# Attention followed by a two-expert layer: four experts of half 0 first, gathered row tiles last, eight store tiles

## The chip, the cores and the metric

The kernel runs on one core of a Trainium2 chip. The metric is the device time of one execution in microseconds. Of the kernel before, four runs are known: 454.48, 451.84, 455.76 and 464.94 us, a median of 455.12 us. One execution was recorded by the hardware profiler; its time is 454.48 us, and the span from its first to its last profiled instruction is 452.6 us, so 1.9 us lie around the span. All times of day below ("at 208.8") are microseconds from the start of that span.

## The reference, cut to what matters

Causal attention in blocks of 64 over q, k, v of 8 batches x 8 heads x 576 positions x 64; its output, with the heads side by side, is x of 4608 tokens x 512. A noisy router picks two of eight experts per token. Each expert is two matrix products with a ReLU between.

```python
attn = softmax(mask(scale * q @ k.T)) @ v          # mask: block_i >= block_j, blocks of 64
x = attn.transpose(0, 2, 1, 3).reshape(B * S, H * D)
noisy = x @ w_gate + log1p(exp(x @ w_noise)) * noise
top2, top2_w = two largest of noisy per token, softmax over the two
for e in range(8):
    for k in range(2):
        mask = top2[:, k] == e
        h = np.maximum(x[mask] @ w1[e], 0.0)        # 512 -> 1024
        out[mask] += top2_w[mask, k, None] * (h @ w2[e])   # 1024 -> 512
```

## The kernel before, in words

**Attention and router.** The batches go in four groups g = 0 to 3 of two batches (1152 tokens, nine tiles of 128 rows). A counter of slots, 26 for a group (UG), paces everything: `at(slot, fn, ...)` files a call, `run(slot)` makes the calls of a slot. Groups 0 and 1 are half 0 of the tokens, groups 2 and 3 half 1. For each group the router gives every token two row numbers, one in each of its two experts' blocks, and `scatter` (L496, an indirect DMA issued by GpSimd, L499) writes a tile of token rows to such rows of a DRAM buffer, `xd[0]` or `xd[1]`: 18 scatters a group. A block has CAP = 640 rows, five row tiles of 128. Rows of tokens for which the expert is the higher-numbered of the two stand at the low end of the block, the others at its high end. `LT[e]` = 0, 1, 2, 3, 3, 4, 5, 5 is how many of expert e's five row tiles, from the low end, may hold rows of the first kind.

**Expert blocks.** Sixteen blocks b = 0 to 15 follow, one for each pair (half, expert), in the order of the list `SEQ` (L626): (0,0) (0,1) (0,2) (1,0) (1,1) (1,2), then (0,3) (1,3) (0,4) (1,4) and so on. "Layer1(b,f)" is `layer1` (L567): eight steps f = 0 to 7 a block, each 4 x 2 matmuls of 320 columns (L574) and one ReLU on ScalarE (L577). "Layer2(b,c)" is `layer2` (L581): five steps c = 0 to 4, one for each row tile, each eight matmuls of 512 columns (L586). The PSUM tile `yp` of such a step is one of two; it is read by ScalarE, which scales it by the router's weight into a tile `ysb` (L591, one of four) that a DMA stores to `yd[half]` (L593); expert 7 has no such store. For c < LT[e] VectorE also reads it: `yo` = yp x weight + `yg` (L596), and an indirect DMA of GpSimd scatters `yo` to the output (L598). `yg` holds the partner rows of the same tokens, fetched from `yd` of the same half by `gather` (L609, an indirect DMA of GpSimd, L614), so it can only be fetched when the stores of all lower experts of the half have landed. Ten `yg` tiles go round.

**Order of the work.** The whole program is in an order written by hand (`steps`, L823): layer1(b,1..7), layer1(b+1,0), layer2(b,0..4), and so on; after every step one more slot is run. What goes with a step:

- `load_x` (L515) reads the block's 640 rows of `xd`, transposed, into `xg` (three tiles) by a DMA on SP's queue (L519). It waits until every scatter of that half has landed. Blocks 0, 1 and 2 are loaded at slots 3*UG+18 to 3*UG+21, block 3 (the first of half 1) at layer1(2,1), block b+2 at layer1(b,1) from there on (`XL`, L833).
- `load_rec` and `read_rec` fetch and work out the row numbers and weights of a half; those of half 1 at layer1(2,1) and layer1(3,3).
- `load_w` (L220, issued at L232) loads one expert's w1 and w2 in four parts k = 0 to 3 of 512 KB, in bf16, by plain DMAs of GpSimd. Experts 0, 1, 2 come during attention and blocks 0 and 1 (pools `wE`, `wM`); expert 3 at blocks 3 and 4, expert 4 at 5 and 6, and so on (`WL`, L813).
- Gathers: block 1's at layer1(1,1); blocks 2 to 8 at steps 2, 3, 4, 6, 7 of the block's own layer 1 (`GJ`); from block 9 on in the block ahead (`GS`).
- The 18 scatters of group 3, the last of half 1, are filed for slots 118 to 135, one a slot, which are the steps of blocks 0 and 1. GpSimd issues scatters, gathers, output scatters and weight loads in one order; each of its DMAs also waits for its eighth predecessor's landing (one of eight semaphores).

Of the kernel before, what the change touches and what calls it, by code (L numbers as in the profile page):

```python
# [9 lines left out]
BF16 = mybir.dt.bfloat16  # L10
# [9 lines left out]
def kernel(  # L20
# [15 lines left out]
    N, Dm = out.shape  # L36
    E = moe_w_gate.shape[1]
    F = moe_w1.shape[2]
    assert Dm == H * D and N == B * S
    P = 128  # L40
# [5 lines left out]
    NH = 2  # L46
    TH = NT // NH
    CAP = 640
    CT = CAP // P
# [8 lines left out]
    LT = (0, 1, 2, 3, 3, 4, 5, 5)  # L58
# [5 lines left out]
    UG = 2 * UN  # L64
# [32 lines left out]
    wE = main.enter_context(tc.tile_pool(name="wE", bufs=2))  # L97
# [6 lines left out]
    top = main.enter_context(ExitStack())  # L104
# [115 lines left out]
    def load_w(pool, e, k=None):  # L220

        if k in (None, 0, "a"):
            wload[e] = (pool.tile([P, DB, F], BF16, tag="w1", name="w1sb"),
                        pool.tile([P, FB, Dm], BF16, tag="w2", name="w2sb"))
        for i, (t, src) in enumerate(zip(wload[e], (moe_w1[e], moe_w2[e]))):
            n = t.shape[1]
            w = src.rearrange("(b p) c -> p b c", p=P)
            if k is None or k == "ab"[i]:
                nc.gpsimd.dma_start(out=t, in_=w)
            elif k in (2 * i, 2 * i + 1):  # L230
                b0 = (k % 2) * n // 2
                nc.gpsimd.dma_start(out=t[:, b0:b0 + n // 2], in_=w[:, b0:b0 + n // 2])  # L232
# [280 lines left out]
    ffn = {}  # L513

    def load_x(b):  # L515
        half, e = SEQ[b]
        assert len(scat[half]) == 2 * TH
        xg = ffn["x"].tile([P, DB, CAP], BF16, tag="xg", name="xg") if b else xa
        ins = nc.sync.dma_start_transpose(out=xg, in_=xd[half][e * CAP:(e + 1) * CAP, 0:Dm])  # L519
        for nm in scat[half]:  # L520
            tc.add_manual_dep(ins.ins, nm, SYNC_DEP, reason="rows landed")
        xgs[b] = xg
# [44 lines left out]
    def layer1(b, fb):  # L567
        half, e = SEQ[b]
        w1sb = wload[e][0]
        hs[b] = hbuf[b % 2]  # L570
        hp = sc_ps.tile([P, 2, 512], F32, tag="sc")
        for db in range(DB):
            for n in range(2):
                nc.tensor.matmul(out=hp[:, n, 0:NW], lhsT=w1sb[:, db, fb * P:(fb + 1) * P],  # L574
                                 rhs=xgs[b][:, db, n * NW:(n + 1) * NW],
                                 start=(db == 0), stop=(db == DB - 1))
        ins = nc.scalar.activation(out=hs[b][:, fb, :].rearrange("p (n w) -> p n w", n=2),  # L577
                                   in_=hp[:, :, 0:NW], func=AF.Relu)
        pace.append(ins.ins.name)

    def layer2(b, c):  # L581
        half, e = SEQ[b]
        w2sb = wload[e][1]
        yp = av_ps.tile([P, Dm], F32, tag="av")
        for fb in range(FB):
            nc.tensor.matmul(out=yp, lhsT=hs[b][:, fb, c * P:(c + 1) * P], rhs=w2sb[:, fb, :],  # L586
                             start=(fb == 0), stop=(fb == FB - 1))
        w = wrow[half][:, e, c:c + 1]
        if e + 1 < E:
            ysb = ffn["y"].tile([P, Dm], BF16, tag="ysb", bufs=4)  # L590
            ins = nc.scalar.activation(out=ysb, in_=yp, func=AF.Copy, scale=w)  # L591
            pace.append(ins.ins.name)
            nc.scalar.dma_start(out=yd[half][e * CAP + c * P:e * CAP + (c + 1) * P, :], in_=ysb)  # L593
        if c < LT[e]:
            yo = ffn["y"].tile([P, Dm], F32, tag="yo", bufs=8)
            nc.vector.scalar_tensor_tensor(out=yo, in0=yp, scalar=w, in1=ygs.pop((b, c)),  # L596
                                           op0=ALU.mult, op1=ALU.add)
            ins = nc.gpsimd.indirect_dma_start(  # L598
                out=out, out_offset=bass.IndirectOffsetOnAxis(ap=trow[half][:, e, c:c + 1], axis=0),
                in_=yo, in_offset=None, bounds_check=N - 1, oob_is_err=False)  # L600
            if outs:
                tc.declare_no_dep(ins.ins, group="out", reason="a token's row is written once")
            tc.add_to_no_dep_group("out", ins.ins)
            outs.append(ins)
# [4 lines left out]
    def gather(b, c):  # L609

        half, e = SEQ[b]
        yg = ffn["yg"][len(gathers) % GB]
# [9 lines left out]
    GJ = (2, 3, 4, 6, 7)  # L622
    GS = (2, 3, 5, 6)


    SEQ = [(0, e) for e in range(3)] + [(1, e) for e in range(3)]  # L626
    for e in range(3, E):
        SEQ += [(0, e), (1, e)]
    NB = len(SEQ)
    todo = {}  # L630

    def at(slot, fn, *args):
        todo.setdefault(slot, []).append((fn, args))

    def run(slot):

        def rank(item):
            fn, args = item
            if fn is router_step:
                return 3 if rgen_n.get(args[0], 0) in (0, 1, 2, 8, 14, 15) else 0  # L640
            return {av_tile: 1, transpose_qk: 2, x_transpose: 2}.get(fn, 4)

        items = todo.pop(slot, [])
        while items:
            items.sort(key=rank)
            fn, args = items.pop(0)
            fn(*args)
# [51 lines left out]

    def read_flags():  # L700
        rs["over"] = nc.values_load(flag_i[0:1, 0:1], min_val=0, max_val=1)

    fl = keep.tile([P, 4, E], F32)
    flm = keep.tile([P, 1], F32)
# [83 lines left out]
    for u in range(NG * UG):  # L788
        if u % 2 == 0:
            score_unit(*divmod(u, UG))  # L790
            score_unit(*divmod(u + 1, UG))
        run(u)
        if u == 3 * UG + 13:
            raws_up.close()
            ffn["x"] = raws_up.enter_context(tc.tile_pool(name="xgp", bufs=3, side="right", reuse_waits="tile"))
            ffn["rec"] = raws_up.enter_context(tc.tile_pool(name="recp", bufs=1, side="right", reuse_waits="tile"))
            wM = raws_up.enter_context(tc.tile_pool(name="wM", bufs=1, side="right", reuse_waits="tile"))
            at(3 * UG + 18, load_x, 0)
            at(3 * UG + 19, load_x, 1)
            at(3 * UG + 20, load_rec, 0)  # L800
            at(3 * UG + 21, load_x, 2)
            for k in range(4):
                at(4 * UG + (8, 10, 13, 16)[k], load_w, wM, 2, k)

    WL = {}

    def open_top(slot):
        if slot == NG * UG + 6:
            top.close()
            wL = top.enter_context(tc.tile_pool(name="wL", bufs=2, reuse_waits="tile"))  # L810
            ffn["y"] = top.enter_context(tc.tile_pool(name="yp", bufs=4, reuse_waits="tile"))
            ffn["yg"] = [ffn["y"].tile([P, Dm], BF16, name=f"yg{i}", bufs=1) for i in range(GB)]
            for i, pool in enumerate((wL, wL, wE, wE, wM)):  # L813
                for k in range(4):
                    WL[3 + 2 * i + k // 2, (2, 6)[k % 2]] = (pool, 3 + i, k)

    slot = NG * UG
    at(slot + 14, read_rec, 0)
    for i in range(GB):
        at(slot + 15 + i, clear_yg, i)  # L820
    at(slot + 80, flags)
    at(slot + 90, read_flags)
    steps = []  # L823
    for b in range(NB):
        steps += [(layer1, b, fb) for fb in range(0 if b == 0 else 1, FB)]
        if b + 1 < NB:
            steps.append((layer1, b + 1, 0))
        steps += [(layer2, b, c) for c in range(CT)]
    for i in range(7):
        run(slot)  # L830
        slot += 1
        open_top(slot)
    XL = {(2, 1): 3, (2, 2): 4}  # L833
    for b in range(3, NB - 2):
        XL[b, 1] = b + 2
    for fn, b, j in steps:
        fn(b, j)
        if fn is layer1:
            if (b, j) in XL:
                load_x(XL[b, j])  # L840
            if (b, j) == (2, 1):
                load_rec(1)
            if (b, j) == (3, 3):
                read_rec(1)
            if (b, j) in WL:
                load_w(*WL[b, j])
            if b == 1 and j == 1:
                gather(b, 0)
            elif 1 < b < 9 and j in GJ and GJ.index(j) < LT[SEQ[b][1]]:
                gather(b, GJ.index(j))  # L850
            if 9 <= b + 1 < NB and j in GS and GS.index(j) < LT[SEQ[b + 1][1]]:
                gather(b + 1, GS.index(j))
        if fn is layer2 and 9 <= b + 1 < NB and j == 0 and LT[SEQ[b + 1][1]] > 4:
            gather(b + 1, 4)
            if b + 1 == NB - 1:
                nc.gpsimd.drain()  # L856
        run(slot)
        slot += 1
        open_top(slot)
# [90 lines left out]
```

## Time and profile before

| what | value |
|---|---|
| four runs | 454.48, 451.84, 455.76, 464.94 us; median 455.12 |
| the profiled execution | 454.48 us, span 452.6 us |
| TensorE matmuls | 406.7 us busy, 90% of the span |
| ScalarE, GpSimd, VectorE | 252.2, 249.0, 157.4 us busy |
| matmuls of layer 1 (960 on `xg`, 64 on `xa`), mean | 300 ns on `xg` (L574) |
| matmuls of layer 2 (624 recorded), mean | 382 ns (L586) |
| software DMA queue (GpSimd's) | 55.78 MB, 75.6% of 16 engines' span |

How to read it: a matmul's own duration overlaps with its neighbour's, so a step's price is read from start to start in the timeline (layer 1: 1.09 us a step, layer 2: 1.72 us). "Idle before, releaser" in a timeline is the time for which the engine stood still ahead of the line and what ended that. The DMA row of the page is the mean busy share of the core's 16 DMA engines. DMAs issued by GpSimd are in queue q0, those of SP in q1, the stores of ScalarE in q10.

### The profile page before, as it was taken

The numbers are of one execution on the slowest core, as the hardware profiler recorded it, in microseconds if no ns is written. First come the engines' busy times: TensorE is split into PE (matmuls) and PEld (weight loads), VectorE is DVE, ScalarE is ACT, GpSimd is POOL, SyncE is SP. The second block draws the span as 40 slices with busy tenths as digits, with TensorE's granted clock in tenths as the row PEclk, the third lists the DMA queues.
The fourth block names the chain that finished last, engine by engine and source line by source line (L and its number), as shares of the span: only waits on it lengthen the run. The fifth ranks groups of instructions, "written<-read, shape, count | busy, mean of one in ns | idle before, by whom it ended". The sixth has DMA issues, their size and how long they took to land. (4 is left out here: it accounts for less than half of the span.)

```text
span 452.6 us, 9810 instructions
## 1 busy us (share of the span) xinstructions
PE 406.7 (90%) x3936; PEld 252.9 (56%) x3952; DVE 157.4 (35%) x508; ACT 252.2 (56%) x343; POOL 249.0 (55%) x297
## 2 busy tenths in 40 slices
PE   2788988988887999875999999999999999999994
PEld 2445755756655766442556556556556566555561
DVE  1576767877868880000300110110110211212212
ACT  2897887788796155341445446455455455455240
POOL 8877361688877786760301243345543746647343
PEclk9969986987987999995999999999999999999998
DMA  8999999999988999549976776987988999945222
GB/s 134 172 136 173 218 194 191 174 253 162 125 185 175 215 212 221 183 142 138 195 163 94 164 176 124 221 171 172 243 177 206 199 227 247 183 147 180 72 85 103
DMA packets 134633, 78.67 MB, mean 174 GB/s; under 512 B 96001, under 2 KB 124419, under 8 KB 134580
## 3 DMA queue, kind: packets, MB, share of 16 engines
q0 software_dynamic: 70368, 55.78, 75.6%
q1 hardware_dynamic: 54132, 13.00, 16.2%
q10 hardware_dynamic: 10080, 9.18, 6.4%
q8 instruction: 33, 0.54, 0.5%
q14 instruction: 20, 0.16, 0.1%
HBM read 68.28 MB, written 33.13 MB: 224 GB/s over the span
## 5 line engine op out<-in xcount | busy, mean ns | idle before, releaser
L574 PE MATMUL hp<-xg,w1sb 128*128 128x320 bf16 x960 | 134.4, 300 | 9.2 <-DMA xg<-xd 8.4
L586 PE MATMUL yp<-w2sb,hq 128*128 128x512 bf16 x624 | 140.3, 382 | 2.5 <-DVE yo L596 1.4
L574 PEld LDWEIGHTS <-w1sb 128*128 128x128 bf16 x1024 | 100.3, 98 | 51.3 <-DMA xg<-xd 8.8
L577 ACT ACTIVATE hq<-hp 128x640 bf16<-128x640 f32 x128 | 90.0, 704 | 67.2 <-PE hp L574 66.4
L596 DVE SCALAR_TENSOR_TENSOR yo<-yp,wrow,yg 128x512 f32<-128x512 f32 x46 | 34.5, 750 | 239.3 <-ACT ysb L591 197.1
L586 PEld LDWEIGHTS <-hq 128*128 128x128 bf16 x640 | 63.1, 99 | 75.9 <-issue 3.8
L302 ACT ACTIVATE esc<-sc 128x1024 bf16<-128x1024 f32 x96 | 92.8, 1023 | 13.4 <-PE sc L299 13.0
L499 POOL DMA_INDIRECT xd<-xr,slots x72 | 71.3, 990 | 36.8 <-issue 15.7
L591 ACT ACTIVATE ysb<-yp,wrow 128x512 bf16<-128x512 f32 x70 | 48.1, 687 | 76.8 <-PE yp L586 73.6
L614 POOL DMA_INDIRECT yg<-yd,orow x46 | 47.4, 1031 | 73.8 <-ACT hq L577 62.9
L598 POOL DMA_INDIRECT out_dram<-yo,trow x46 | 45.7, 994 | 67.4 <-DVE yo L596 53.6
L299 PE MATMUL sc<-hq 64*128 64x512 bf16 (+4 forms) x320 | 39.9, 345 | 13.3 <-ACT esc L302 10.8
L341 PE MATMUL av<-vt,esc 128*128 128x65 bf16 x640 | 35.3, 215 | 6.0 <-DVE xr L360 4.7
L212 POOL DMA_DIRECT2D vt<-in_v_dram x40 | 34.0, 867 | 10.0 <-PE av L355 6.3
L341 PEld LDWEIGHTS <-esc 128*128 128x128 bf16 x640 | 28.4, 111 | 16.7 <-DVE xr L360 9.4
L360 DVE TENSOR_TENSOR xr<-av,rden 128x256 bf16<-128x256 f32 x72 | 30.6, 424 | 2.6
L299 PEld LDWEIGHTS <-hq 64*128 64x128 bf16 x320 | 13.1, 101 | 26.5 <-issue 16.8
L256 PE MATMUL tp<-ident,raw 128*64 128x128 bf16 x512 | 24.6, 251 | 2.6 <-DMA raw<-in_q_dram 2.3
L269 ACT ACTIVATE hq<-tp 128x1024 bf16<-128x1024 bf16 (+1 forms) x20 | 17.0, 851 | 14.8 <-PE tp L259 8.0
L256 PEld LDWEIGHTS <-raw 128*64 128x64 bf16 x512 | 18.7, 128 | 8.3 <-issue 3.7
L262 DVE COPY hq<-tp 128x1024 bf16<-128x1024 bf16 (+1 forms) x24 | 14.3, 598 | 9.4 <-PE tp L256 6.2
L359 DVE RECIPROCAL rden<-av 128x4 f32<-128x4 f32 x72 | 12.8, 178 | 9.4 <-PE av L341 5.6
(122 smaller groups left out, 218.6 us busy)
## 6 DMA issues: line engine op xcount, KB each, us to landing
yd<-ysb ACTq DMA_DIRECT2D x70, 128.0 KB, 4.8
w1sb<-in_moe_w_dram POOLq DMA_DIRECT2D x16, 512.0 KB
w2sb<-in_moe_w_dram POOLq DMA_DIRECT2D x16, 512.0 KB
vt<-in_v_dram POOLq DMA_DIRECT2D x32, 128.0 KB
raw<-in_q_dram POOLq DMA_DIRECT2D x9, 256.0 KB
raw<-in_k_dram POOLq DMA_DIRECT2D x9, 256.0 KB
xd<-zero SPq DMA_DIRECT2D x16, 132.0 KB, 3.9
raw<-in_q_dram POOLq DMA_DIRECT2D x1, 1152.0 KB
```

Of the source, the lines that this page charges most:

```text
L256: nc.tensor.transpose(to[64 * hf:64 * hf + 64, :, r, :], raw[:, (t0, t1)[hf], r * 64:(r + 1) * 64], ident)
L299: nc.tensor.matmul(out=sc[:, hf, off:off + z - a], lhsT=kT[sl, c0 + jt * P:c0 + jt * P + P], rhs=qT[sl, c0 + a:c0 + z], start=True, stop=True)
L302: ins = nc.scalar.activation(out=esc[:, hh, :, piece * 512:(piece + 1) * 512], in_=sc, func=AF.Exp, scale=scale)
L341: nc.tensor.matmul(out=av[:, hh, :], lhsT=esc[:, hh, hf, c:c + P], rhs=vb[:, 4 * hf + jt, st * SET + hh, :], start=(jt == 0), stop=(jt == ib))
L499: ins = nc.gpsimd.indirect_dma_start(out=xd[half].bitcast(I32), out_offset=bass.IndirectOffsetOnAxis(ap=slots[:, g * TG + idx, i:i + 1], a ...
L574: nc.tensor.matmul(out=hp[:, n, 0:NW], lhsT=w1sb[:, db, fb * P:(fb + 1) * P], rhs=xgs[b][:, db, n * NW:(n + 1) * NW], start=(db == 0), sto ...
L577: ins = nc.scalar.activation(out=hs[b][:, fb, :].rearrange("p (n w) -> p n w", n=2), in_=hp[:, :, 0:NW], func=AF.Relu)
L586: nc.tensor.matmul(out=yp, lhsT=hs[b][:, fb, c * P:(c + 1) * P], rhs=w2sb[:, fb, :], start=(fb == 0), stop=(fb == FB - 1))
L591: ins = nc.scalar.activation(out=ysb, in_=yp, func=AF.Copy, scale=w)
L596: nc.vector.scalar_tensor_tensor(out=yo, in0=yp, scalar=w, in1=ygs.pop((b, c)), op0=ALU.mult, op1=ALU.add)
L598: ins = nc.gpsimd.indirect_dma_start(out=out, out_offset=bass.IndirectOffsetOnAxis(ap=trow[half][:, e, c:c + 1], axis=0), in_=yo, in_offse ...
L614: ins = nc.gpsimd.indirect_dma_start(out=yg, out_offset=None, in_=yd[half][0:e * CAP, :], in_offset=bass.IndirectOffsetOnAxis(ap=orows[hal ...
```

## The change

1. `SEQ` begins with four experts of half 0, then four of half 1: (0,0) (0,1) (0,2) (0,3) (1,0) (1,1) (1,2) (1,3), then (0,4) (1,4) and so on in turn. The first block of half 1 is block 4 instead of block 3.
2. `load_x` of block 3, now (0,3), is filed for slot 3*UG+22, after the three others. Block 4 (half 1) is loaded at layer1(2,1), `load_rec(1)` at layer1(3,1), `read_rec(1)` at layer1(4,3).
3. The four loads of expert 3's weights go to slots 4*UG+20, 23, 26, 29, that is into the steps of blocks 0 and 1. Experts 4 to 7 come at blocks 4 and 5, 6 and 7, 8 and 9, 10 and 11.
4. `order(b)` runs the row tiles of layer 2 from LT[e] to 4 first and 0 to LT[e]-1 after them.
5. `ysb` has eight tiles instead of four.
6. Gathers move to the block ahead from block 8 on. In the condition for the earlier blocks the lower bound is gone: for blocks 1 and 5 (LT = 1) both branches hold, at step 1 and at step 2, so their one gather is issued twice, into two `yg` tiles, and the second is the one that is read. There are 48 gathers instead of 46.

In GpSimd's program the last scatters of half 1 stood as: gather (1,0), eight scatters, output scatter (1,0), three scatters, two gathers. Now: w1 of expert 3 (first half), gather, scatter, gather, two scatters, w1 (second half), three scatters, w2, three scatters, w2, two scatters, output scatter (1,0), two gathers.

```diff
         if e + 1 < E:
-            ysb = ffn["y"].tile([P, Dm], BF16, tag="ysb", bufs=4)
+            ysb = ffn["y"].tile([P, Dm], BF16, tag="ysb", bufs=8)
...
-    SEQ = [(0, e) for e in range(3)] + [(1, e) for e in range(3)]
-    for e in range(3, E):
+    E1 = 4
+    SEQ = [(h, e) for h in range(NH) for e in range(E1)]
+    for e in range(E1, E):
         SEQ += [(0, e), (1, e)]
...
+    pools = {}
+
+    def load_later(e, k):
+        load_w(pools["wL"], e, k)
...
             at(3 * UG + 21, load_x, 2)
+            at(3 * UG + 22, load_x, 3)
             for k in range(4):
                 at(4 * UG + (8, 10, 13, 16)[k], load_w, wM, 2, k)
+                at(4 * UG + (20, 23, 26, 29)[k], load_later, 3, k)
...
-            for i, pool in enumerate((wL, wL, wE, wE, wM)):
+            for i, pool in enumerate((wL, wE, wE, wM)):
                 for k in range(4):
-                    WL[3 + 2 * i + k // 2, (2, 6)[k % 2]] = (pool, 3 + i, k)
+                    WL[4 + 2 * i + k // 2, (2, 6)[k % 2]] = (pool, 4 + i, k)
...
+    def order(b):
+
+        n = LT[SEQ[b][1]]
+        return [*range(n, CT), *range(n)]
+
...
-        steps += [(layer2, b, c) for c in range(CT)]
+        steps += [(layer2, b, c) for c in order(b)]
...
-    XL = {(2, 1): 3, (2, 2): 4}
-    for b in range(3, NB - 2):
-        XL[b, 1] = b + 2
+    XL = {(b, 1): b + 2 for b in range(2, NB - 2)}
...
-            if (b, j) == (2, 1):
+            if (b, j) == (3, 1):
                 load_rec(1)
-            if (b, j) == (3, 3):
+            if (b, j) == (4, 3):
                 read_rec(1)
...
-            if b == 1 and j == 1:
+            if b in (1, E1 + 1) and j == 1:
                 gather(b, 0)
-            elif 1 < b < 9 and j in GJ and GJ.index(j) < LT[SEQ[b][1]]:
+            elif b < 2 * E1 and j in GJ and GJ.index(j) < LT[SEQ[b][1]]:
                 gather(b, GJ.index(j))
-            if 9 <= b + 1 < NB and j in GS and GS.index(j) < LT[SEQ[b + 1][1]]:
+            if 2 * E1 <= b + 1 < NB and j in GS and GS.index(j) < LT[SEQ[b + 1][1]]:
                 gather(b + 1, GS.index(j))
-        if fn is layer2 and 9 <= b + 1 < NB and j == 0 and LT[SEQ[b + 1][1]] > 4:
+        if fn is layer2 and 2 * E1 <= b + 1 < NB and j == order(b)[0] and LT[SEQ[b + 1][1]] > 4:
             gather(b + 1, 4)
```

## The prediction, made before the changed kernel ran

> **What bounds the kernel now.** I read the page's slices first, then the timeline of TensorE where its row dips, then what each wait there hangs on.
>
> Busy tenths of TensorE, its granted clock and the DMA engines, 40 slices of 11.3 us:
>
> ```profile
> PE   2788988988887999875999999999999999999994
> ...
> PEclk9969986987987999995999999999999999999998
> DMA  8999999999988999549976776987988999945222
> ```
>
> From slice 20 on TensorE is full and its clock whole, so the expert blocks can only be shortened where matmuls are missing. That is one dip, slices 17 to 19 (192 to 226 us). The timeline of TensorE (start, length, idle before and its releaser) shows it:
>
> ```profile
> 182.59 3.40 PE L586 MATMUL yp<-w2sb,hq 128*128 128x512 bf16 x15
> 187.43 5.34 PE L586 MATMUL yp<-w2sb,hq 128*128 128x512 bf16 x24 [1.45 <-DVE yo L596]
> 192.61 7.77 PE L574 MATMUL hp<-xg,w1sb 128*128 128x320 bf16 x56
> 208.82 2.32 PE L574 MATMUL hp<-xg,w1sb 128*128 128x320 bf16 x8 [8.44 <-DMA xg<-xd]
> 210.93 0.63 PE L586 MATMUL yp<-w2sb,hq 128*128 128x512 bf16 x1
> 211.78 9.53 PE L586 MATMUL yp<-w2sb,hq 128*128 128x512 bf16 x38 [0.22 <-issue]
> 221.15 8.86 PE L574 MATMUL hp<-xg,w1sb 128*128 128x320 bf16 x64
> 230.06 8.58 PE L586 MATMUL yp<-w2sb,hq 128*128 128x512 bf16 x39
> 238.48 6.82 PE L574 MATMUL hp<-xg,w1sb 128*128 128x320 bf16 x49
> ```
>
> An undisturbed block is 238.48 - 221.15 = 17.33 us (layer 1 1.09 a step, layer 2 8.58 in all). Layer1(3,0), the first step of half 1, could start at 200.38 and starts at 208.82. The next two stretches are slow as well. By stretches of 5 us (TensorE busy, ..., clock, DMA share, GB/s):
>
> ```profile
> 195.00:200.00 5.00, 5.00 (x39) 3.60 (x38) 0.00 (x0) 3.47 (x5) 3.78 (x5) 1.00 0.32 118
> 200.00:205.00 5.00, 0.38 (x3) 0.04 (x1) 0.00 (x0) 0.74 (x2) 1.98 (x2) 0.89 0.77 136
> 205.00:210.00 5.00, 1.18 (x5) 0.73 (x6) 0.00 (x0) 0.00 (x0) 0.00 (x0) 0.50 1.31 91
> 210.00:215.00 5.00, 4.78 (x16) 2.08 (x16) 0.00 (x0) 1.26 (x2) 0.00 (x0) 0.59 0.96 182
> ```
>
> After the wait the clock is 0.50 and 0.59. From 200.38 to 221.15 pass 20.77 us for work of 1.09 + 8.58 = 9.67: **11.10 us lost**, 8.44 of waiting and 2.66 of slow matmuls. What it waits for is GpSimd's stream of scatters:
>
> ```profile
> 181.88 0.97 POOL L499 DMA_INDIRECT xd<-xr,slots  x1 [2.54 <-DMA xd<-xr,slots]
> 183.16 1.07 POOL L614 DMA_INDIRECT yg<-yd,orow  x1 [0.30 <-issue]
> ...
> 198.63 0.97 POOL L499 DMA_INDIRECT xd<-xr,slots  x1 [0.30 <-issue]
> ```
>
> The last scatter of half 1 is issued until 199.60, and only then can the transposing load of block 3 start; it lands 9.22 us later. GpSimd goes without a break there (0.30 us between DMAs), so this date is set by how many DMAs it issues. Two smaller losses: layer2(1) takes 192.61 - 182.59 = 10.02 instead of 8.58, **1.44 us**, since its first tile's PSUM waits for `yg`; and at 394 us the four `ysb` tiles run out: ScalarE waits 2.06 us for a store, and TensorE for ScalarE, by the waits (total, times, longest):
>
> ```profile
> PE hp L574 <- ACT hq L577: 0.7, 1, 0.7
> ```
>
> That is **0.7 us** of TensorE. All that the change can win is 11.10 + 1.44 + 0.7 = 13.2 us.
>
> **The change part by part.**
>
> *Block order.* Block 3 is now (0,3), whose rows landed before 150; its load is the third after that of block 1. Block 4 is the first that needs half 1. With no stall, layer1(4,0) comes 12.54 us earlier than its 221.15 + 7 x 1.09 = 228.78 of before: at 216.24. The question is what lands by then, and whether expert 3's w1 is there at 200.38 - 1.44 = 198.94, when layer1(3,0) now starts.
>
> *Load of block 3 moved up (SP's queue, q1).* It now runs at about 165, when the engines are full. Prices from the DMA queues (packets, MB, share of 16 engines), of one load in 230 to 234 and of weight parts in 221 to 230:
>
> ```profile
> q1 hardware_dynamic: 2592, 0.66, 81.8%
> ```
>
> ```profile
> q0 software_dynamic: 1028, 1.50, 97.9%
> ```
>
> A load is 0.818 x 4 = 3.3 us of all 16 engines; a weight part of 512 KB is 0.524 / 1.50 x 8.8 = 3.1 us. The 2.54 us wait of GpSimd before 181.88 shows that it is held by landings there, so I take the whole 3.3 us as delay of GpSimd: the scatter of 181.88 goes to 185.2. Bounds: 0, if the scatters have room, and 3.3.
>
> *Weights of expert 3 moved up (GpSimd's queue, q0).* Four issues of 0.80 us each stand ahead of the last scatters: 3.2 us. The extra gather adds 1.28, the output scatter that now stands behind the scatters takes 1.28 away. Last scatter: 198.63 + 3.3 + 3.2 = 205.1, issued until 206.1; plus 9.22, landing at 215.3. But the last weight part, issued until 203.5, and two scatters are in the same queue: 203.5 + 3.1 + 2 x 0.37 = 207.3, later than the issue by 1.2 (0.37: in 184 to 200 q0 moved 1.75 MB in 30.4% of 16 us, and a scatter is 0.135 MB). **Block 4 lands at 216.5**, against 216.24: 0.3 us of stall, I take 0.5. The four parts are 12.4 us of engine time, put into 185 to 207, where the engines were under half used (0.32 in 195 to 200): that is their cover, and without it they would come on top. Bounds of the landing: 212.0 (no delay by the load: no stall) and 220.7 (loads here take up to 10.0 us from issue to landing instead of 8.4: +1.6; another wait like that of 2.54 on GpSimd).
>
> w1 of expert 3: scatter of 185.2, first part until 187.0, two gathers and three scatters of 1.28, second part until 194.2; with 3.1 us and about 1 us to start it lands at 198.3, against 198.94 and, for its half of the sum, 0.5 later. No cost; its lateness would run beside that of block 4's load, not add to it.
>
> By the Trainium skill, "DMA: Bandwidth & Descriptors", section "Anatomy of one DMA — SWDGE (gpsimd) path", a DMA moves its bytes at 436 GB/s beside a fixed 2.0 us, which would make a queued part 1.2 us. The row says 3.1 at a 97.9% busy queue; by the page there would be no backlog at all and the sum would be 0.5 us lower. The row decides.
>
> *Order of the row tiles.* Block 1's gathered tile is now the fifth. Its second gather is issued at about 190.9 and lands 3.4 us later (183.16 to VectorE's start at 186.6): 194.3. The tile is ready at 191.2; its PSUM is wanted again only in layer2(2) at 200: the 1.44 us go, with 5 us to spare. Late next is block 2: its gathers now stand behind the scatters, issued until 210, landing at 213; its two gathered tiles are its last, and their PSUM is wanted at 217.7. Block 3's gathers wait behind block 2's output scatters and land near 222.5; wanted at 225. In the old order blocks 2 and 3 would stall here; this part is needed for the first.
>
> *Eight `ysb`.* Takes the 0.7 us. *Second extra gather* (block 5): 1.3 us of GpSimd, hidden in its waits (62.6 us for layer 1 after 225). *Other weights* come one block earlier against their use or as before: nothing. The tail (452.6 - 446.4 after the last tile) moves along.
>
> Sum against the profiled execution: 454.5 - 11.10 - 1.44 - 0.7 + 0.5 = 441.8 us. That execution is 0.64 us below the median, so 442.4 us is my forecast beside 455.12.
>
> **The rivals.**
>
> *The load of half 1 is still late, by part.* Landing at 220.7: a stall of 4.5 us, and slow matmuls after it in proportion to before (2.66 for 8.44), 1.4. 442.4 + 5.9 - 0.5 = 447.8. For: the engines are full from 150 to 184, and two more loads follow at once. Against: the half-empty DMA row at 185 to 200. By the Trainium skill, "TensorE: Matmul & The Clock Gate", Part 1, the clock halves after an idle window of about 3.4 us, and so a stall of 4.5 us would cost 1.7 more and one of 0.5 nothing. No row here shows where between 1.45 us (clock 1.00 after it) and 8.44 us it begins.
>
> *The wait moves one block on, whole.* Block 4 would have to land at 216.24 + 8.44 = 224.7; then only 13.2 - 11.1 = 2.1 us are won: 453.0, no change that can be told. It takes 8 us more delay than the sum has; nothing in the rows gives it.
>
> *Slower: expert 3's weights become the bound.* They stand in GpSimd's one stream behind scatters and gathers that wait. Each us after 198.94 costs one; from 212.1 on the change loses, and 1% is lost at 216.7. For: the margin is only 0.6 us. Against: 13 us of delay is five times the longest wait of GpSimd in that stretch (2.54). If it came, landing at 217: 460.
>
> **How the numbers follow.** My forecast 0.70 (own range 440.5 to 445), partly late 0.18, wait moved 0.07, slower by weights 0.05. The range reaches from the landing at 212.0 and a little shortened block (440.5) past the second case to 449.5; the other two, 0.12, and the edges are out. A measurement of this kernel tells about 1% from no change, 4.6 us. Both first cases are faster by more: 0.88; within 1% 0.07; slower 0.05.
>
> **What would show it.** Right: no idle TensorE of 1.45 at 187 and of 8.44 at 200; layer1(4,0) starting at 216 to 218; last scatter issued near 206; clock 1.00 in 200 to 215; no wait of `ysb` on its store. Wrong: an idle stretch before layer1(3,0) released by `w1sb` (weights), one of over 4 us before layer1(4,0) released by `xg` (load), or one in layer2(2) or (3) released by `yo` (gathers).

## The result and the profile after

The changed kernel took 453.76 us in the median of twelve runs (445.31 to 467.97) where the kernel before took 454.48 in seventeen (451.41 to 464.94). The ratio of the two is 0.985, 95% interval 0.980 to 0.991. The ratio leaves out runs more than 1.5% above the fastest of their kernel, here seven of the twelve (452.28 to 467.97) and one of the seventeen, and the profiled one, of 455.25 us (span 453.5), is among the seven, with stops of TensorE that the change itself made. Between the medians of all runs no change can be told. So the kernel can be 1.5% faster, and something in it goes wrong often.

Slices of the page of the changed kernel (11.3 us each):

```profile
PE   2788987978978998798499999999999999999994
...
PEclk9959989989988999899599999999999999999998
DMA  8999999999987999899957689999999999844222
```

The dip of TensorE has not gone. It has moved from slices 17 to 19 to slice 19, with a small one at 16. Timeline of TensorE, the same stretch as that shown of before:

```profile
177.79 2.20 PE L574 MATMUL hp<-xg,w1sb 128*128 128x320 bf16 x15
183.56 1.25 PE L574 MATMUL hp<-xg,w1sb 128*128 128x320 bf16 x4 [3.56 <-DMA w1sb<-in_moe_w_dram]
185.02 9.34 PE L586 MATMUL yp<-w2sb,hq 128*128 128x512 bf16 x39 [0.22 <-issue]
194.19 8.86 PE L574 MATMUL hp<-xg,w1sb 128*128 128x320 bf16 x64
202.89 8.80 PE L586 MATMUL yp<-w2sb,hq 128*128 128x512 bf16 x39
211.52 2.34 PE L574 MATMUL hp<-xg,w1sb 128*128 128x320 bf16 x16
222.03 9.35 PE L574 MATMUL hp<-xg,w1sb 128*128 128x320 bf16 x48 [8.18 <-ACT hq L577]
231.22 8.80 PE L586 MATMUL yp<-w2sb,hq 128*128 128x512 bf16 x39
239.85 1.39 PE L574 MATMUL hp<-xg,w1sb 128*128 128x320 bf16 x9
```

The waits of 1.45 us (in layer2(1)) and of 8.44 us (before layer1(3,0)) are gone. In their place stand two that nobody expected: 3.56 us before layer1(2,0), for the second part of expert 2's w1, and 8.18 us inside layer 1 of block 3, a block of half 0 whose rows had landed long before; it waits for ScalarE. From 211.52 to 239.85 pass 28.33 us for a block of 17.33: 11.00 us lost, as much as the 11.10 that the change was to save. The ReLUs of layer1(1,0) and layer1(2,0) stand 21.6 us apart instead of 17.3, so the first stop costs 4.3; 0.9 go in the slow matmuls after it. That is 16.2 us, against 13.7 lost in before (by the same count). Attention had ended 2.0 us earlier in this execution, which hides most of the difference.

What ScalarE was doing, from its timeline (ACTq lines are the DMAs that it issues):

```profile
210.71 0.33 ACTq L593 DMA_DIRECT2D yd<-ysb  x1
211.72 0.69 ACT L591 ACTIVATE ysb<-yp,wrow 128x512 bf16<-128x512 f32 x1 [1.04 <-PE yp L586]
220.91 0.33 ACTq L593 DMA_DIRECT2D yd<-ysb  x1
221.28 1.30 ACT L577 ACTIVATE hq<-hp 128x640 bf16<-128x640 f32 x2 [8.87 <-DMA xg<-xd]
```

The fifth tile of layer2(2) is ready at 212.41, its store should be issued at once like the four ahead of it, and is issued at 220.91; the ReLUs of block 3 stand behind it in ScalarE's one stream. The releaser named is the transposing load of **block 4**, which no ReLU of block 3 reads. In the built program the reason is plain: the DMAs of SP and of ScalarE share eight semaphores that are handed out in turn, and this store got the one that block 4's load had taken. It waits until that load has landed. The waits say the same (total, times, longest):

```profile
ACT hq L577 <- DMA xg<-xd: 8.9, 1, 8.9
...
PE hp L574 <- ACT hq L577: 8.2, 1, 8.2
```

So a load that is due at layer1(4,0) stops TensorE two steps of layer 1 into block 3. And the load is late: GpSimd's timeline,

```profile
161.28 0.79 POOL L232 DMA_DIRECT2D w1sb<-in_moe_w_dram  x1
...
169.29 1.02 POOL L499 DMA_INDIRECT xd<-xr,slots  x1 [0.31 <-ACT ysb L591]
179.72 0.97 POOL L499 DMA_INDIRECT xd<-xr,slots  x1 [9.41 <-ACT hq L577]
...
187.62 0.97 POOL L499 DMA_INDIRECT xd<-xr,slots  x1 [2.25 <-DMA w2sb<-in_moe_w_dram]
...
207.80 0.98 POOL L499 DMA_INDIRECT xd<-xr,slots  x1 [0.30 <-issue]
```

shows the last scatter issued at 207.80 instead of the 205.1 of the prediction. GpSimd stood still 9.41 us before 179.72. Its eighth predecessor there is the first part of expert 2's w1, issued at 161.28. TensorE waits until 183.56 for the second part, issued at 166.03 and landed at 183.51. Both were on their way beside the load of block 3. DMA queues from 163 to 178 us (packets, MB, share of 16 engines):

```profile
q0 software_dynamic: 837, 1.61, 71.9%
q1 hardware_dynamic: 2599, 0.65, 33.6%
```

One transposing load (2560 packets) was spread over these 15 us and took 5.0 us of all engines; in before the load of block 3 took 4.8 of all engines, over 5.3 us, and the one at 230 us took 3.3. That this load kept the weights from landing is not shown. By the counts of their semaphores, 14 of the first part's 16 shares had landed by 169.73, the next at 172.81 and the last only at 178.95; of the second part 15 had landed by 179.64 and the last at 183.51. One share of sixteen was late each time, and no record says why.

### The profile page after: what moved, and what is told of

It reads as the page before. It is cut to its first block, busy times and chain, and to the rows that moved or that the text cites. A ratio compares the mean times of both kernels' runs of the same rounds, so it can differ in the third digit from the quotient of the medians.

```text
span 453.5 us, 9810 instructions
## 1 busy us (share of the span) xinstructions
PE 404.4 (89%) x3936; PEld 251.3 (55%) x3952; DVE 158.3 (35%) x508; ACT 251.9 (56%) x343; POOL 251.2 (55%) x299
## 3 DMA queue, kind: packets, MB, share of 16 engines
q1 hardware_dynamic: 54132, 13.00, 19.2%
## 5 line engine op out<-in xcount | busy, mean ns | idle before, releaser
L574 PE MATMUL hp<-xg,w1sb 128*128 128x320 bf16 x960 | 136.5, 304 | 11.7 <-ACT hq L577 8.2
L614 POOL DMA_INDIRECT yg<-yd,orow x48 | 49.5, 1032 | 56.2 <-ACT hq L577 26.4
L299 PE MATMUL sc<-hq 64*128 64x512 bf16 (+4 forms) x320 | 38.3, 330 | 12.8 <-ACT esc L302 10.3
L341 PE MATMUL av<-vt,esc 128*128 128x65 bf16 x640 | 33.7, 209 | 7.9 <-DVE xr L360 6.3
L341 PEld LDWEIGHTS <-esc 128*128 128x128 bf16 x640 | 26.9, 107 | 18.0 <-DVE xr L360 12.1
L269 ACT ACTIVATE hq<-tp 128x1024 bf16<-128x1024 bf16 (+1 forms) x20 | 17.0, 851 | 13.4 <-PE tp L256 6.7
```

What stands on the lines that cost most here:

```text
L299: nc.tensor.matmul(out=sc[:, hf, off:off + z - a], lhsT=kT[sl, c0 + jt * P:c0 + jt * P + P], rhs=qT[sl, c0 + a:c0 + z], start=True, stop=True)
L341: nc.tensor.matmul(out=av[:, hh, :], lhsT=esc[:, hh, hf, c:c + P], rhs=vb[:, 4 * hf + jt, st * SET + hh, :], start=(jt == 0), stop=(jt == ib))
L614: ins = nc.gpsimd.indirect_dma_start(out=yg, out_offset=None, in_=yd[half][0:e * CAP, :], in_offset=bass.IndirectOffsetOnAxis(ap=orows[hal ...
```

## The experiments

Three pairs of reasons were open: what stops block 3 (the shared semaphore, or simply the late rows of half 1), what the load of block 3 does at 163 us, and why TensorE, full from 240 us on in the profile above, stops late in the kernel in other executions. The runs fell on several chips. On two of them everything is slower (the kernel before takes 491.53 or 484.16 us there, and the first ReLU of layer 1 comes at 184 to 188 us instead of 156), so a number is only set beside its own kernel before.

### First set: one part of the change at a time

**Old tile order in the changed kernel.**

```diff
-        steps += [(layer2, b, c) for c in order(b)]
+        steps += [(layer2, b, c) for c in range(CT)]
```

> The changed kernel with the row tiles of layer 2 in the old order 0 to 4; all else of the change stays. The prediction's theory: the gathers of block 2 are issued behind the last scatters and land 10 us or more after its first gathered tile, which now comes first, so TensorE stops in layer2(2) by some 9 us (released by yo), and a part of that takes the place of the wait for half 1; the time is 2 to 9 us above the changed kernel. Rival: the wait for half 1 ends as late in any case and covers it all, and the time is that of the changed kernel within 1 us.

490.09 us beside 491.53, ratio 1.005 (1.001 to 1.010). TensorE stops for 2.18 us in layer2(1) and 1.23 in layer2(2), both for gathered rows, and not for 9; layer2(3) has no stop. The size was wrong, and so was the place, by one block. Layer 1 begins 27 us later on this chip than in the profile of before (first ReLU at 183.64 and not at 156.42), and the changed kernel itself was not run here, so what the old order costs it on this chip is not measured.

**Tile order alone, in the kernel before.**

```diff
-        steps += [(layer2, b, c) for c in range(CT)]
+        n = LT[SEQ[b][1]]
+        steps += [(layer2, b, c) for c in [*range(n, CT), *range(n)]]
```

> The kernel before with the new order of the row tiles alone. The prediction's theory: only the 1.44 us wait in layer2(1) goes, the wait for half 1 starts earlier and ends at the same time of day, so 0 to 1.5 us below the kernel before. Rival: the tile order is what makes the changed kernel faster, and this one is as fast as that, 1.5% below the kernel before (6 to 7 us).

505.59 us beside 491.53, ratio 1.039 (1.031 to 1.048): the expectation missed, and this part alone makes the kernel slower. Beside a stop of 7.84 us at 235 in layer1(2,3), for a ReLU, there are stops of 3.57 us at 328 and of 5.86 at 407, where the profile of before shows none. These two are for ReLUs as well: ScalarE, ahead of them, waits 17.6 us in five waits for stores of `ysb`, of which this kernel has only four tiles, and the loads of blocks 9 and 13 are on their way for 15.4 and 13.4 us there. This is the first sign of what the third set looks at.

**Load of block 3 behind layer1(1,2)**, and **second half of expert 3's weights behind the last scatter:**

```diff
-            at(3 * UG + 22, load_x, 3)
...
+            if (b, j) == (1, 2):
+                load_x(3, pace[-1])
```

> The changed kernel, with the load of block 3's rows held until the ReLU of layer1(1,2), at about 175 us, instead of following block 2's load at 160. Theory A: that load meets the weights of expert 2 and the scatters while the DMA engines are full and delays both by more than the 3.3 us of the prediction; held back, the wait for expert 2's w1 before layer1(2,0) (3.6 us in the profile) goes, GpSimd has no stop of 9 us near 170 to 180, the last scatter is issued by about 204 and the time falls by 3 to 6 us, to 441 to 444. Theory B: the delay of half 1 comes from expert 3's weights in GpSimd's queue; then the time stays within 1 us of the changed kernel.

```diff
-                at(4 * UG + (20, 23, 26, 29)[k], load_later, 3, k)
+                at(4 * UG + (20, 23, 32, 33)[k], load_later, 3, k)
```

> The changed kernel, with the two loads of expert 3's w2 filed behind the last scatter instead of among the last ones. Theory B: the last scatter is issued 1.6 us earlier and has one or two weight parts of 3.1 us less ahead of it in the queue, so block 4's rows land 2 to 4 us earlier and the time falls by as much. Theory A: the delay arises earlier, between 165 and 185; the time falls by 1.6 us at most.

486.61 us (476.61 to 508.38) and 496.48 (483.91 to 497.85) beside 491.53. The spread is wider than any of the effects, and neither gives an interval: inconclusive as times. In the profiles block 3 of the first takes 24.1 us and block 2 of the second 24.3, and TensorE waits for ReLUs there. In the first a store of `ysb` was held 4.06 us by the load of block 4, as in the changed kernel; in the second no store is held at that place, and the profile names no cause.

### Second set: the semaphore, and the load of block 3

**The changed kernel once more, on the chip of this set.**

> The changed kernel once more, as the base of this set. All theories: TensorE's stop in block 3 stands at layer1(3,3), not at layer1(4,0), released by ScalarE, and its end is the landing of block 4's rows; its length follows that landing (8.2 us in the first profile).

469.38 us in the median of six, from 443.22 to 483.72, beside 453.0 (no interval). The profiled one stops 4.43 us in block 3 for a ReLU, as above, and then late: 1.85, 3.07, 5.92 and 3.15 us in layer 2 between 336 and 416 us, all released by `yo`.

**The load of block 4 placed behind the ReLU of layer1(3,0)**, so that it gets a later turn of the eight semaphores, and no store that precedes that ReLU can wait for it:

```diff
-    XL = {(b, 1): b + 2 for b in range(2, NB - 2)}
+    XL = {(b, 1): b + 2 for b in range(3, NB - 2)}
...
+            if (b, j) == (3, 0):
+                load_x(4, pace[-1])
```

> The changed kernel, with block 4's load placed behind the ReLU of layer1(3,0) in the order in which the eight semaphores of SP's and ScalarE's DMAs are given out; it starts no earlier, since it waits for the last scatter anyway. Theory S: in the changed kernel the fifth store of block 2 has the semaphore of block 4's load and waits for its landing on ScalarE's queue, with the ReLUs of block 3 behind it; here no store of block 2 does. TensorE then runs on to layer1(4,0), the stop shrinks to what the load is late there (0 to 3 us), no slow clock follows, and the time is 4 to 10 us below the changed kernel. Rival L: the rows are late by as much at layer1(4,0), the stop only moves there with its length, and the time stays within 1 us.

Timeline of TensorE, blocks 2 to 4:

```profile
196.84 8.80 PE L588 MATMUL yp<-w2sb,hq 128*128 128x512 bf16 x39
205.47 8.86 PE L576 MATMUL hp<-xg,w1sb 128*128 128x320 bf16 x64
214.17 8.80 PE L588 MATMUL yp<-w2sb,hq 128*128 128x512 bf16 x39
222.80 8.86 PE L576 MATMUL hp<-xg,w1sb 128*128 128x320 bf16 x64
```

No wait at all: 222.80 - 205.47 is 17.33, and blocks 1 to 10 all take that. The fifth store of layer2(2) goes out at once, at 206.39, and packets of the load of block 4 are still moving at 210.58: the load no longer holds it. The last scatter is earlier here too, at 198.57, so part of the 8.18 us would have gone without the new turn; but in the changed kernel the load landed at 220.9, where layer1(4,0) would have begun at 219.15 had nothing stopped, and without the shared semaphore it would have cost about 1.8 us (an estimate from these two times). The stop in block 3 was for the most part the semaphore. The shortest of six runs is 442.52, 0.1 us from the prediction's sum; the median is 453.25 beside 453.0 (no interval), since a late stop is there in this profile too, 7.59 us in layer2(11).

**The same with block 3's load behind layer1(1,2)**, and **with the double gathers and the weight delay taken out as well:**

```diff
+            if (b, j) == (1, 2):
+                load_x(3, pace[-1])
...
-            elif b < 2 * E1 and j in GJ
+            elif b not in (1, E1 + 1) and b < 2 * E1 and j in GJ
...
-                at(4 * UG + (20, 23, 26, 29)[k], load_later, 3, k)
+                at(4 * UG + (20, 23, 32, 33)[k], load_later, 3, k)
```

> As e6, and block 3's load is held until the ReLU of layer1(1,2). Theory A: that load at 160 to 178 us delays expert 2's w1 (3.6 us of TensorE before layer1(2,0) in the first profile) and the scatters behind it; then 2 to 5 us below e6. Rival: the wait for w1 was chance; within 1 us of e6.

> As e7, and the two loads of w2 of expert 3 stand behind the last scatter, and the gathers of blocks 1 and 5 are issued once. The last scatter is then issued about 2.9 us earlier than in e7 (two issues of 0.8 and a gather of 1.3). If block 4's load is still late in e7, the time falls by up to that; if nothing is late there, it is the same within 1 us. By the sum of the prediction without any stall it is 13 us below the kernel before.

454.51 us, ratio 0.986 (0.978 to 0.993), and 461.08, ratio 1.006 (1.001 to 1.012). The theory that the load only has to come later fell. In the first of the two it is on its way from 182 to 198 us and takes 81.3% of those 17 us on all engines, 13.8 us, four times its price alone, because it now meets expert 3's weights and the scatters; TensorE stops for those weights (timeline),

```profile
202.22 0.72 PE L576 MATMUL hp<-xg,w1sb 128*128 128x320 bf16 x4 [1.06 <-DMA w1sb<-in_moe_w_dram]
207.36 1.25 PE L576 MATMUL hp<-xg,w1sb 128*128 128x320 bf16 x4 [4.42 <-DMA w1sb<-in_moe_w_dram]
```

and the last scatter goes to 212.3. In the second these stops are 7.28 and 3.80 us, and 5.43 before layer1(4,0) for its load: the one rival that made the kernel slower, expert 3's weights, is real once they meet a transposing load.

### Third set: transposing loads that meet GpSimd's transfers

What a late stop looks like, in the run with block 4's load in another turn. TensorE, ScalarE and VectorE, GpSimd, and stretches of 5 us (the last three columns are clock, DMA share, GB/s), in this order:

```profile
367.44 3.21 PE L588 MATMUL yp<-w2sb,hq 128*128 128x512 bf16 x8 [7.59 <-DVE yo L598]
```

```profile
356.44 0.69 ACT L593 ACTIVATE ysb<-yp,wrow 128x512 bf16<-128x512 f32 x1 [1.04 <-PE yp L588]
365.55 0.33 ACTq L595 DMA_DIRECT2D yd<-ysb  x1
365.92 0.69 ACT L593 ACTIVATE ysb<-yp,wrow 128x512 bf16<-128x512 f32 x1 [8.80 <-DMA xg<-xd]
366.64 0.75 DVE L598 SCALAR_TENSOR_TENSOR yo<-yp,wrow,yg 128x512 f32<-128x512 f32 x1 [8.73 <-ACT ysb L593]
```

```profile
346.24 0.97 POOL L600 DMA_INDIRECT out_dram<-yo,trow  x1 [0.96 <-DVE yo L598]
361.32 0.80 POOL L232 DMA_DIRECT2D w2sb<-in_moe_w_dram  x1 [14.11 <-DMA yg<-yd,orow]
```

```profile
340.00:345.00 5.00, 5.00 (x27) 2.53 (x26) 2.08 (x3) 2.06 (x3) 2.81 (x4) 1.00 1.10 77
345.00:350.00 5.00, 5.00 (x39) 3.59 (x38) 0.75 (x1) 3.10 (x5) 1.25 (x2) 1.00 1.27 53
350.00:355.00 5.00, 4.95 (x32) 3.02 (x32) 0.00 (x0) 2.83 (x5) 0.00 (x0) 1.00 1.28 69
```

TensorE waits for VectorE, VectorE for ScalarE, and ScalarE for the issue of a store, ready at 357.13 and issued at 365.55: the shared semaphore again, this time taken by the load of block 13. Other late stops have another end: before the stops of 5.92, 3.15 and 3.07 us of the first run of the second set VectorE waited 15.76, 13.17 and 9.77 us for gathered rows. GpSimd's 14.11 us is a wait for a gather, issued at 335.63, to land. What these stops have in common is a transfer that is long on its way. In the 15 us of the stretches the DMA engines are more than fully busy (shares over 1 are overlapping packets) and move 53 to 77 GB/s; from 335 to 365 us of the last run below they move 202 on the mean. What is on its way is one load of `xg`, issued at 334.56: queue q1 from 337 to 358 us,

```profile
q1 hardware_dynamic: 2555, 0.65, 67.8%
```

is 14.2 us of all engines, against 3.3 for the load at 230 us of before. The theory: a transposing load that meets GpSimd's transfers, weight parts above all, slows both, and everything behind them is late. By the theory, the tile order brings the two together. With the gathered tiles last, the output scatters wait for the end of layer 2, and the weight part behind them in GpSimd's order is issued 11.4 us after the ReLU of layer1(b,0), or later, where it was 6 to 10 in before; the load is issued at 16.2 in both, when its `xg` tile comes free. These times are of the first of a block's two weight parts. The second came at 14.7 to 15.5 us in blocks 5 to 7 of before, close ahead of loads that still took only 2.9 to 4.5 us of the engines, so a near issue alone does not make a load long. Three kernels on one chip test this.

**Old tile order, with the load of block 4 in the other turn:**

```diff
-        steps += [(layer2, b, c) for c in order(b)]
+        steps += [(layer2, b, c) for c in range(CT)]
...
+            if (b, j) == (3, 0):
+                load_x(4, pace[-1])
```

> The changed kernel with the load of block 4 behind ReLU(3,0), and with the old order of the row tiles (0 to 4). Theory (the late stops come from the tile order: with the gathered tiles last, GpSimd's output scatters wait until the end of layer 2 and hold the weight parts behind them, which are then issued 11.4 us after the ReLU of layer1(b,0) and meet the transposing load issued at 16.2; in the old order they were issued 6 to 10 us after it): weight parts at 6 to 10 us again, the transposing loads of blocks 8 to 15 at most 5.5 us long, no stop of TensorE over 1 us after 300 us. Stops of 2 to 9 us in layer 2 of blocks 2 and 3, released by yo, as the prediction said of the old order. Time 444 to 451. Rival (the late stops have nothing to do with the tile order: they come from the order of the experts, or by chance): loads of 7 to 20 us and a late stop of 5 to 9 us as before this edit, 452 to 465.

**New tile order, the loads of blocks 7 to 15 moved to 7 us after that ReLU:**

```diff
+        if fn is layer2 and 4 <= b < NB - 3 and j == order(b)[3]:
+            load_x(b + 3, pace[-1])
```

> The changed kernel with the load of block 4 behind ReLU(3,0), new tile order kept, and the transposing loads of blocks 7 to 15 issued behind the fourth row tile of layer 2, about 7 us after the ReLU of layer1(b,0), between the weight parts issued at 11.4 to 20 and those of the next block. Each still comes more than 25 us ahead of its use. Theory (a transposing load that meets a weight part slows itself and everything behind it in GpSimd's queue): loads of blocks 7 to 15 at most 6 us long, no stop of TensorE over 1 us after 235 us, all blocks 17.33 us, 441 to 444. Rival (the long loads are a sign of something else that crowds the DMA engines late in the kernel, gathers and stores among it): some loads stay over 7 us, a stop of 3 to 9 us by yo stays, median 447 to 455.

**The same move in the kernel before, where it brings them to the weight parts:**

```diff
+        if fn is layer2 and 4 <= b < NB - 3 and j == 3:
+            load_x(b + 3, pace[-1])
```

> The kernel before with the same edit: the transposing loads of blocks 7 to 15 issued behind the fourth row tile of layer 2, about 7 us after the ReLU of layer1(b,0). In this kernel the weight parts are issued 6 to 10 us after that ReLU, so here the edit brings the two together. Theory: loads of blocks 7 to 15 of 6 to 20 us, stops of TensorE late in the kernel released by yo, 3 to 10 us in all, slower than the kernel before by 0.5 to 2.5%, 457 to 466 where that has 454. Rival (the loads come 25 us ahead of their use, and nobody waits for them): no change, 453 to 455.

The kernel before took 484.16 us on this chip.

*Old order:* 483.27 us, ratio 1.001 (0.996 to 1.005). The late stops after 340 us are gone, and all sixteen loads take 15.3% of a span of 481.7, that is 73.7 us of the engines (73.3 in before, 107.8 in the run above). One load still met a part of w1, issued at 292.82 us, and TensorE stopped 2.88 us behind it. The old order has its price one block ahead of the place that the prediction named:

```profile
218.57 7.03 PE L588 MATMUL yp<-w2sb,hq 128*128 128x512 bf16 x24 [3.47 <-issue]
...
239.55 5.34 PE L588 MATMUL yp<-w2sb,hq 128*128 128x512 bf16 x24 [1.81 <-DVE yo L598]
```

These are layer2(1) and layer2(2); layer2(3) runs without a stop. In the next run, with the new order on the same chip, layer2(1) and layer2(2) run through in 8.80 us each. The twelve runs of this kernel lie within 1.9% (479.39 to 488.48), where those of the changed kernel spread over 5%.

*The loads moved:* 501.14 us, slower by 17 than before (no interval), and the expectation missed. The loads of blocks 7, 8 and 9 are as short as wanted (first to last packet 3.2, 3.1 and 3.5 us). The next, at 329 us, met a part of w1 issued at 328.09 and took 12.5 us of the engines in 18. From block 8 on the gathers stand one block ahead, GpSimd's order is another, and there is no gap at 7 us. The remedy was wrong; that load agrees with the theory.

*The loads moved in the kernel before:* 510.62 us beside 484.16 (no interval, but the lowest of six, 499.34, is above the highest of seventeen, 492.53). A load that is needed 25 us later made the kernel 26 us slower. Page, slices of 12.9 us:

```profile
PE   3888888687877779959999999598959966986894
```

and queue q1 from 315 to 334 us, one load, 11.1 us of all engines:

```profile
q1 hardware_dynamic: 2583, 0.66, 58.6%
```

The rival (nobody waits for the loads) is out. The loads are long more often where they are moved onto the transfers, but not always: of the nine moved, five are on their way for 9.4 to 20.7 us (blocks 9, 10, 11, 13 and 15) and four for 3.1 to 4.7, where in before the nine take 2.5 to 6.6. What decides it is open. Nor is it gathered rows alone that TensorE waits for. Three of its stops are behind `yo` (4.07, 1.17 and 2.50 us), but the two longest, 5.44 and 8.91, are for ReLUs behind ScalarE, which waits 22.4 us in six waits for stores of its four `ysb` tiles.

**Last run: the new order only where it is needed.**

```diff
     def order(b):
 
-        n = LT[SEQ[b][1]]
+        n = LT[SEQ[b][1]] if b < 2 * E1 else 0
         return [*range(n, CT), *range(n)]
```

with the load of block 4 in the other turn.

> The changed kernel with the load of block 4 behind ReLU(3,0), and the new order of the row tiles only in blocks 0 to 7; from block 8 on, where the gathers come in the block ahead, the old order 0 to 4. Theory (the tile order is needed where the gathers of a block stand in its own layer 1, and from there on only pushes the weight parts onto the transposing loads): transposing loads 10 to 15 at most 5.5 us long, no stop of TensorE over 1 us after 235 us and none in blocks 2 and 3, blocks of 17.33 us throughout; 441 to 445 where the kernel before has 454, or 471 to 476 where it has 484, that is a ratio of 0.970 to 0.982. Rival (long loads come late in the kernel in either order, from the weights of experts 4 to 7 coming a block earlier): two or more loads of 7 to 20 us after 300 us, stops of 3 to 9 us by yo, ratio 0.985 to 1.01.

449.06 us (443.57 to 455.79, six runs) beside 453.7, ratio 0.984 (0.976 to 0.993). From 240 us on there is not one stop of TensorE over 0.4 us, and a load late in the kernel looks like this (q1 from 343 to 348 us, 4.9 us):

```profile
q1 hardware_dynamic: 2591, 0.66, 98.2%
```

Slices of the page, and the one stop that is left:

```profile
PE   2788988988877999999699999999999999999994
```

```profile
206.21 7.77 PE L576 MATMUL hp<-xg,w1sb 128*128 128x320 bf16 x56
217.71 2.31 PE L576 MATMUL hp<-xg,w1sb 128*128 128x320 bf16 x8 [3.73 <-DMA xg<-xd]
```

That is layer1(4,0) waiting for its own load: the prediction's second case, the load of half 1 late by part. With the slow matmuls after it, it costs 6.4 us (two blocks of 22.29 and 18.77). The expectation missed by little: a ratio of 0.984 for at most 0.982, and 6.7 us on its way for the load of block 10. The ratio is within its interval that of the changed kernel; what seems gained is in the median of all runs, 449.1 against 453.8, and in the longest, 455.8 against 468.0, though from six runs and twelve, on two chips.

## Why the prediction was right, and where it was wrong

It was right in the direction and in the range: 0.985 of 455.12 is 448.4, inside 440.5 to 449.5. It was not right in its likeliest number, 442.4, which single runs reach (443.57 and 442.52 with small mends, 443.22 as it is) and the middle of the runs does not. Part of the hit is luck: the upper part of the range was there for a late load of half 1, and losses of other kinds filled it. The median of all twelve runs, 453.76, lies outside.

- *11.10 us before layer1(3,0), 1.44 in layer2(1), 0.7 for `ysb`.* All three are gone from the trace, as said. What came instead was not among the rivals in this form: the wait moved, by a semaphore, to a place where no data are needed. The nearest rival, "the wait moves one block on, whole", had about the size (8.18 for 8.44) and about the time of this execution (453.0 for 455.25), but not the cause.
- *Load of block 3: at most 3.3 us of delay for GpSimd.* This term was too small first. It priced the load by the engine time that it takes alone, and took the two transfers to share the engines without loss. The load took 5.0 us of engine time, in before 4.8, but was on its way for 15.2 us, where GpSimd stood still 9.41 us and TensorE 3.56. In three other runs with the same load in place it took 8.7, 5.3 and 3.2 us from first to last packet, GpSimd's longest wait there was 3.75, 2.37 and 1.71 us, and TensorE did not stop. So the load and the waits grow together; which of them is the cause, or whether the late shares of the weight parts are, no run shows.
- *Last scatter at 205.1, landing 9.22 + 1.2 us after its issue.* Measured 207.80, or 53.4 us after the ReLU of layer1(0,0), against 48.7 in the prediction; in the three other runs with the tile order and block 3's load in place, on chips as fast as this one, 44.7 to 48.9 us. That term was well sized where block 3's load was short. From the end of the issue to the landing it took 12.1 us here and 13.7 in the last run, not 10.4. Expert 3's weight parts in the same queue delay the last rows by more than 1.2 us: with them ahead, the load of half 1 is issued 7.5 us after the last scatter here and 7.0 in the second set's run with block 3's load moved, and 1.8 in its neighbour on the same chip, where the second half of the weights stands behind the scatters (the double gathers are out there too). The rows of block 4 were in at 220.9 instead of 216.5: 2.7 us by the later scatter and 1.7 by the landing.
- *Expert 3's w1 in time for layer1(3,0).* Right; no wait for it in the changed kernel.
- *Order of the tiles.* Needed, but for blocks 1 and 2 (3.47 and 1.81 us there without it, 2.18 and 1.23 on the slower chip) and not for 2 and 3. That it costs something later was not considered at all.
- *"Other weights come one block earlier against their use or as before: nothing."* This failed second, and cost the most in the profiled run of the second set. The sum asked when each transfer is due, and not what it runs beside. The tile order moved the first weight parts in GpSimd's stream from 6 to 10 us to 11.4 and later, towards loads that stayed where they were; with the order kept for half 0 alone, or left out, the late stops but one go. The profiled run of the second set stops for 1.85 + 3.07 + 5.92 + 3.15 us.
- *The clock.* The prediction said that no row shows from which stop on it falls. Now rows do, and no single length of stop decides it: after stops of 1.81, 1.85 and also 3.15 us (until 415.05 in the first run of the second set) it stays 1.00, after 2.88, 3.47 and 3.73 the stretch of 5 us shows 0.66, 0.73 and 0.60, and after one of only 2.18 us, in the run with the old tile order, the 3.4 us from 217.9 show 0.50. In these traces the clock changes only at steps of 3.41 us. Of the stops of 2.18 and 3.73 us 2.09 and 2.00 lay within one step; the one of 1.81 lay in one step whole; the one of 3.15 was split over two, 1.57 and 1.58. The page "TensorE: Matmul & The Clock Gate" of the Trainium skill, Part 1, puts the fall at an idle window of about 3.4 us: the length agrees with the steps of 3.41 us, but 2.0 us of idling within one were enough here, and the measurement decides. The second case's price, 4.5 + 1.4 us, came out as 3.73 + 2.67.

What stays open: whether it is the weight parts or the gathers and scatters in GpSimd's queue that hurt a transposing load most (the long ones met both); why single shares of a weight part land late; and how the 6.5 us that are missing (6.7 us gained, 13.2 forecast) divide among the semaphore, the stop at 183 us and the late loads, since none of the shorter runs of the changed kernel has a profile.

## What to carry to other kernels

Ask of every DMA that is moved what it will be in flight with, not only when it must land; a transposing load beside another queue's transfers had here up to four times its price alone. When a wait names a transfer that the waiting instruction does not read, look for a shared semaphore and give the transfer another turn in the order. A reordering that helps one phase (here the blocks whose gathers stand in their own layer 1) is best tried on that phase alone.

## What the hardware showed that was not expected

- DMA engines at a share of 1.27 with 53 GB/s, in a stretch with one transposing load of 0.66 MB among weight parts and gathers; a share near 1 is no sign that bytes move.
- The sum over all sixteen loads varied from 73 us of engine time (before; old order) to 120.5 (26.2% of 460.1 us, in the run with blocks 3 and 4 loaded later) for the same 54132 packets and 13.00 MB of that queue.
- A store on ScalarE's queue held 8.5 us by a load on SP's queue (212.41 to 220.91), with no data in common.
